# Seven block products: low parts of w_out2 on GpSimd, one weight difference kept in its block's place

## The chip, the cores and the metric

The kernel runs on one core of a Trainium2 chip. The metric is device time in microseconds (us), from the first to the last instruction plus what lies around the program. The engines are named as the profile names them: PE (TensorE matmuls), PEld (its weight loads), DVE (VectorE), ACT (ScalarE), POOL (GpSimd) and SP (the queue that issues DMAs).

## The reference

Three stages in a row: attention with a mask of hash buckets, a bilinear block, and a gated block. The change lies in the third.

```python
# attention: 2 batches x 8 heads, 768 positions, head size 64 -> x of 1536 x 512
h = (x @ w1) * (x @ w2) @ w3;  x = h @ w_out                 # d_ff 1024
gate = 1 / (1 + exp(-(x @ w_gate)));  val = x @ w_val        # d_ff 1536
return (gate * val) @ w_out2                                 # 1536 x 512
```

The inputs are drawn as double precision and are brought to 32 bits on the chip.

## The kernel before

**Precision.** A matrix operand is split into a high part (a rounded copy made by ACT) and a low part (the operand minus the high part, one subtraction of two SBUF operands). A product of two operands is three matmuls: high by high, high by low, low by high. `three` (L705) issues them, `split_w` (L699) and `low` (L778) make the two parts.

**The gated block** is computed for three sweeps of 512 tokens, each over twelve tiles of 128 hidden units. The first sweep multiplies plainly. The last two go through `sevens`, which takes two tiles at a time (a *pair*; six pairs a sweep, twelve in all) and makes each 2 by 2 block product of weights and tokens with seven block products in place of eight, for `w_gate` (k = 0) and `w_val` (k = 1). It needs sums and differences of weight blocks. With B11 and B21 the two blocks of a pair's even tile, and B12 and B22 those of its odd tile:

- `t1` makes B12 - B11 on DVE, into a scratch tile `r1`;
- `t24` makes B22 - (B12 - B11), and B21 minus that, in a scratch tile (`r24`, shown as `xlf`), and splits the two (`wh`, `wl`);
- `t3` makes B22 - B12 (also shown as `xlf`) and splits it and B22 (`da`, `dr`);
- `t1low` splits `r1`, both k in one step of 128x512 (`st`);
- `own` splits the even tile itself (`wah`, `wal`, `wbh`, `wbl`).

The low parts of all of these are made on POOL, the differences themselves on DVE. The seven products of a pair go to halves of the PSUM tiles `pa` and `pb`, and DVE adds each to sums in SBUF (`add`, L882; tiles `a` and `xhf`), which frees the bank for a later product. A gated tile is finished by L945 or L965 (value times gate), a high part on ACT (`gh`) and a low part on DVE (`gl`, L922).

**The second matmul** (`second`, tiles `m`) multiplies a gated tile by its 128 rows of w_out2, four token blocks of three matmuls each. These steps are spread between the seven products. The w_out2 rows are split just before: the high part `wth` on ACT, the low part `wtl` on DVE (L699, since `split_w` is called with `eng=dve`), two buffers.

**Order.** The weights lie in SBUF from the first sweep on (tiles `xall`, `w1r`, `w2r` and `wc`, each in reused space), and nothing is loaded any more in the last two sweeps. Within each engine the instructions stand in a fixed order, which a scheduler lays out from the written order, priorities and its own estimate of times; an instruction whose operands are late holds up what stands behind it on its engine. The work for pair p + 1 is written between the products of pair p.

Of the kernel before, what the change touches and what calls it, by code (L numbers as in the profile page):

```python
# [10 lines left out]
F32 = mybir.dt.float32  # L11
# [218 lines left out]
def lsh_attention_moe_moe2_kernel(  # L230
# [22 lines left out]
    P = 128  # L253
# [8 lines left out]
    CH = 512  # L262
# [8 lines left out]
    dve = nc.vector  # L271
    pool = nc.gpsimd
# [3 lines left out]
    def act_copy(dst, src):  # L276
        act.activation(out=dst, in_=src, func=AF.Copy)  # L277

    def f(ap):
        return ap.bitcast(F32)  # L280
# [409 lines left out]
    def split_w(pl, nm, src, bufs=2, eng=pool):  # L690
        hi = pl.tile([P, DM], F32R, tag=nm + "h", name=nm + "h", bufs=bufs)
        lo = pl.tile([P, DM], F32R, tag=nm + "l", name=nm + "l", bufs=bufs)
        shp = src.shape
        h3, l3 = hi, lo
        if len(shp) == 3:
            h3 = hi.rearrange("p (k f) -> p k f", k=shp[1])
            l3 = lo.rearrange("p (k f) -> p k f", k=shp[1])
        act_copy(h3, src)
        eng.tensor_tensor(out=l3, in0=src, in1=f(h3), op=ALU.subtract)  # L699
        return hi, lo  # L700
# [11 lines left out]
    def ftile(fi):  # L712

        ck, o = divmod(fi, KC)
        g = xall[:, o, ck * CH:(ck + 1) * CH].rearrange("p (k f) -> p k f", k=KC)
        if fi < NF1:
            return g, late["w1"][fi], late["w2"][fi].rearrange("p k f -> p (k f)")
        return g, wc[:, fi - NF1].rearrange("p (k f) -> p k f", k=KC), wc[:, fi - NF1 + KC]

    def moe(psM):  # L720


        tiles = [(1, s, fi) for s in range(1, NSW) for fi in range(NF1)] + [(2, s, fi) for s in range(NSW) for fi in range(NF2)]
        mp, mw = late["mp"], late["mw"]
# [51 lines left out]
        def low(eng, hi, lo, src):  # L776
            act_copy(hi, src)
            eng.tensor_tensor(out=lo, in0=src, in1=f(hi), op=ALU.subtract)  # L778
# [22 lines left out]
        def sevens():  # L801
# [3 lines left out]
            NS = NF2 // 2  # L805
            pairs = [(s, NF1 * (NSW - 1) + s * NF2 + 2 * i) for s in range(1, NSW) for i in range(NS)]
# [4 lines left out]
            h1 = [sts[3][:, i * DM:(i + 1) * DM] for i in range(2)]  # L811
# [5 lines left out]
            h24 = [[mw.tile([P, DM], F32R, tag=t, name=t, bufs=3) for t in ("wh", "wl")] for _ in range(3)]  # L817
            hb3 = [[pl.tile([P, DM], F32R, tag=t, name=t, bufs=b) for t in ("da", "dr")] for pl, b in ((mp, 2), (mp, 2), (dec, 1))]
            W = [{}, {}]
            r1, r24 = (mp.tile([P, CH], F32, tag="o", name="tmp", bufs=2) for _ in range(2))  # L820
            r24 = [r24, None]

            def raw(p, k):
                fi = tiles[pairs[p][1]][2]
                return [fl(t) for t in (ftile(fi)[k][:, 0:2], ftile(fi + 1)[k][:, 0:2], ftile(fi)[k][:, 2:4], ftile(fi + 1)[k][:, 2:4])]

            def sub(o, a, b):
                dve.tensor_tensor(out=o, in0=a, in1=b, op=ALU.subtract)  # L828

            def t1(p):  # L830

                if p < len(pairs):
                    for k in range(2):
                        b11, b12, _, _ = raw(p, k)
                        sub(r1[:, k * 2 * P:(k + 1) * 2 * P], b12, b11)

            def t24(p, k):

                if p < len(pairs):
                    _, _, b21, b22 = raw(p, k)  # L840
                    h, l = h24[(2 * p + k) % 3]
                    r = r24[k]
                    sub(r[:, :2 * P], b22, r1[:, k * 2 * P:(k + 1) * 2 * P])
                    sub(r[:, 2 * P:], b21, r[:, :2 * P])
                    low(pool, h, l, r)
                    W[p % 2][k, 6], W[p % 2][k, 4] = [[half(t, i) for t in (h, l)] for i in range(2)]

            def t3(p, k):

                if p < len(pairs):  # L850
                    _, b12, _, b22 = raw(p, k)
                    h, l = hb3[(2 * p + k) % 3]
                    r = r3[:, k * 2 * P:(k + 1) * 2 * P]
                    sub(r, b22, b12)
                    low(pool, h[:, :2 * P], l[:, :2 * P], r)
                    low(pool, h[:, 2 * P:], l[:, 2 * P:], b22)
                    W[p % 2][k, 7], W[p % 2][k, 3] = [[half(t, i) for t in (h, l)] for i in range(2)]

            def t1low(p):
                if p < len(pairs):  # L860
                    low(pool, *h1, r1)
                    for k in range(2):
                        W[p % 2][k, 5] = [half(t, k) for t in h1]

            def own(p, k):
# [6 lines left out]
            def product(p, k, i):  # L872

                q = (7 * p + place[i]) % 4
                r = banks[k][q % 2][:, q // 2 * 2 * P:(q // 2 + 1) * 2 * P]
                w, x = W[p % 2][k, i], X[i]
                for kk in range(2):
                    three(r, [t[:, kk] for t in w], [t[:, kk] for t in x], kk == 0, kk == 1)
                return r
# [9 lines left out]
            xf = [mw.tile([P, KC, CH], F32, tag=t, name=t + "f") for t in ("xh", "xl")]  # L889
# [4 lines left out]
            t24(0, 1)  # L894
            t3(0, 1)
            t1low(0)
            r1, r24[0] = xf[0][:, 2], xf[1][:, 0]
            yield
            banks = [[psM.tile([P, 512], F32, tag=t, name=t) for t in ("pa", "pb")] for _ in range(2)]
            todo = [(pairs[0][1] - 1, c) for c in range(4)]  # L900
# [1 line left out]
            for p, (s, n) in enumerate(pairs):  # L902
                if p == NS:
                    X = {**nextX, **S}
                elif p == NS - 2:
                    nextX, nextS = blocks(2, [xf[0][:, 3], xf[1][:, 3]] + [mp.tile([P, CH], F32, tag="o", name="tmp", bufs=2) for _ in range(2)])

                def renew(i):
                    if p == NS - 1:
                        low(dve, *S[i], nextS[i])  # L910
                A = [mp.tile([P, CH], F32, tag="a", name="a", bufs=2) for _ in range(2)]
                C = [A, vs]

                def sec():
                    if todo:
                        second(*todo.pop(0))

                def gate(i):
                    gh = mw.tile([P, CH], F32R, tag="gh0", name="gh", bufs=2)
                    gl = mw.tile([P, CH], F32R, tag="gl0", name="gl", bufs=2)  # L920
                    act_copy(gh, vs[i])
                    dve.tensor_tensor(out=gl, in0=vs[i], in1=f(gh), op=ALU.subtract)  # L922
                    gs[n + i] = gh, gl

                for k in range(2):
                    act_copy(C[k][0][:, hi2], product(p, k, 1))
                for k in range(2):
                    add(C[k][1][:, lo2], product(p, k, 6), C[k][0][:, hi2])
                renew(6)
                sec()  # L930
                if p:
                    wts[n - 1] = split_w(mp, "wt", ftile(tiles[n - 1][2])[2], eng=dve)
                for k in range(2):
                    add(C[k][0][:, lo2], product(p, k, 2), C[k][0][:, hi2])
                sec()
                for k in range(2):
                    add(C[k][1][:, hi2], product(p, k, 7), C[k][1][:, lo2])
                renew(7)
                own(p + 1, 0)
                sec()  # L940
                for k in range(2):
                    add(C[k][0][:, hi2], product(p, k, 4), C[k][1][:, hi2])
                    if k == 0:
                        act.activation(out=A[0], in_=A[0], func=AF.Sigmoid)
                dve.tensor_tensor(out=vs[0], in0=vs[0], in1=A[0], op=ALU.mult)  # L945
                gate(0)
                own(p + 1, 1)
                t1(p + 1)
                t24(p + 1, 0)
                sec()  # L950
                wts[n] = split_w(mp, "wt", ftile(tiles[n][2])[2], eng=dve)
                sec()
                for k in range(2):
                    r = product(p, k, 5)
                    add(C[k][1][:, hi2], r, C[k][1][:, hi2])
                    add(C[k][1][:, lo2], r, C[k][1][:, lo2])
                renew(5)
                t3(p + 1, 0)
                sec()
                t24(p + 1, 1)  # L960
                for k in range(2):
                    add(C[k][1][:, lo2], product(p, k, 3), C[k][1][:, lo2])
                    if k == 0:
                        act.activation(out=A[1], in_=A[1], func=AF.Sigmoid)
                dve.tensor_tensor(out=vs[1], in0=vs[1], in1=A[1], op=ALU.mult)  # L965
                gate(1)
                sec()
                t3(p + 1, 1)
                t1low(p + 1)
                sec()  # L970
                todo = [(n + i, c) for i in range(2) for c in range(4)]
            n = pairs[-1][1] + 1
# [5 lines left out]
        gs, wts = {}, {}  # L978
# [40 lines left out]
    o = D // 2  # L1019
# [120 lines left out]
```

## Time and profile before

| what | value |
|---|---|
| median of three runs | 833.38 us (832.77 to 836.6) |
| the profiled execution | 834.98 us, span 833.2 us |
| granted PE clock over the span | 0.995 |
| PE busy | 795.7 us (96%) |
| DVE busy | 669.3 us (80%) |
| ACT busy | 546.3 us (66%) |
| POOL busy | 414.7 us (50%) |

Busy times are unions of an engine's instructions. A group of equal instructions has its number, its mean duration and the idle time of the engine just ahead of it with what ended that idle time. The first sweep of the gated block ends and `sevens` begins its preparations at about 602 us; the products of its first pair start at 621 us, and the last matmul ends at 829.3 us.

### The profile page before, as it was taken

The page shows a single profiled execution, that of the slowest core. Times are in us where ns is not written, and L with a number is a line of the kernel's source. Part 1 is how long each engine was busy: PE and PEld are TensorE (multiplying, and loading weights), DVE is VectorE, ACT ScalarE, POOL GpSimd, SP SyncE. Part 2 cuts the span into 40 slices and gives each one's busy share as a digit, 9 for nine tenths or more (in the row PEclk, how much of TensorE's full clock was granted, in tenths as well). Part 3 has the DMA queues.
Part 4 walks back from the last instruction along what each step waited for, and adds up shares of the span by engine and source line. Part 5 has one row for each costly group of instructions (what it writes and reads, how often), then busy time and mean ns, then how long its engine had stood idle before and what let it go on. Part 6 is the DMA issues. An engine that isn't in the chain of part 4 may idle for free.

```text
span 833.2 us, 13347 instructions
## 1 busy us (share of the span) xinstructions
PE 795.7 (96%) x4576; PEld 684.3 (82%) x4576; DVE 669.3 (80%) x1217; ACT 546.3 (66%) x1085; POOL 414.7 (50%) x420
## 2 busy tenths in 40 slices
PE   6898999999999999999999999999998999899998
PEld 5677888888788888888888888888877889798996
DVE  6869989888799989977376545686799988988874
ACT  6888878777787888876455645656545455555542
POOL 3466443232565464438344434446557566656640
PEclk9999999999999999999999999999999999999999
DMA  6866645344455545130022213334101000010001
GB/s 230 209 193 174 184 121 157 88 121 121 116 140 148 137 124 147 61 111 1 1 77 76 77 52 125 103 113 141 50 1 52 1 1 1 1 52 1 1 1 52
DMA packets 45956, 74.19 MB, mean 89 GB/s; under 512 B 6336, under 2 KB 32960, under 8 KB 45888
## 3 DMA queue, kind: packets, MB, share of 16 engines
q1 hardware_dynamic: 45888, 73.34, 30.3%
q8 instruction: 36, 0.59, 0.3%
q14 instruction: 32, 0.26, 0.1%
HBM read 52.43 MB, written 3.19 MB: 67 GB/s over the span
## 4 chain that ended last, share of the span: by engine, by line
PE 60%; DVE 22%; ACT 6%; issue 6%; DMA 3%; POOL 2%; SPq 0%; ACTq 0%; DVEq 0%; POOLq 0%
PE m L705 11%; PE pa L705 10%; PE pb L705 10%; PE av L541 7%; PE tp L523 4%; PE wacc L600 4%; PE p L705 4%; DVE s L479 3%; PE s L469 3%; PE s L472 2%; PE y L705 2%; DVE pt L528 2%; DVE da L338 2%; DVE xlf L828 2%; PE gps L402 2%
## 5 line engine op out<-in xcount | busy, mean ns | idle before, releaser
L523 PE MATMUL tp<-idf,e 128*128 128x128 f32 x576 | 102.9, 276 | 5.3 <-DVE pt L528 4.9
L336 POOL TENSOR_SCALAR da<-da 128x512 f32<-128x512 f32 x76 | 52.5, 693 | 111.5 <-ACT da L334 110.3
L490 ACT ACTIVATE e<-s,sm 128x768 f32<-128x768 f32 x96 | 95.7, 999 | 15.9 <-DVE sm L480 15.4
L526 ACT ACTIVATE pt<-tp 128x384 fp32r<-128x384 f32 (+1 forms) x192 | 89.9, 493 | 20.7 <-PE tp L523 18.3
L479 DVE TENSOR_REDUCE s<-s 128x1 f32<-128x768 f32 x96 | 91.2, 955 | 11.9 <-PE s L472 10.7
L528 DVE TENSOR_TENSOR pt<-tp,pt 128x384 fp32r<-128x384 f32 x168 | 87.9, 548 | 4.1 <-ACT pt L526 2.9
L523 PEld LDWEIGHTS tp<-idf,e 128*128 128x128 f32 x576 | 71.4, 141 | 19.3 <-DVE pt L528 6.3
L541 PE MATMUL av<-pt,spv 128*128 128x256 f32 (+1 forms) x576 | 85.2, 297 | 1.7 <-DVE pt L528 1.5
L334 ACT ACTIVATE da<-st 128x512 f32<-128x512 f32 x76 | 51.1, 672 | 52.7 <-DVE w1r L343 20.2
L541 PEld LDWEIGHTS av<-pt,spv 128*128 128x128 f32 (+1 forms) x576 | 72.7, 182 | 11.0 <-DVE pt L528 2.4
L469 PE MATMUL s<-bk,bq 128*128 128x384 f32 x192 | 62.8, 389 | 6.4 <-ACT e L490 6.1
L600 PE MATMUL wacc<-wo,t 128*128 128x512 f32 x192 | 64.1, 415 | 1.7 <-DVE pt L528 1.6
L338 DVE SCALAR_TENSOR_TENSOR da<-st,da 128x512 uint32<-128x512 uint32 x76 | 59.6, 785 | 1.2
L705 PE MATMUL m<-wth,gh 128*128 128x512 f32 x144 | 57.4, 399 | 3.0 <-ACT gh L277 2.9
L705 PE MATMUL m<-wtl,gh 128*128 128x512 f32 x144 | 57.1, 396 | 0.0
L472 PE MATMUL s<-ak,aq 128*128 128x384 f32 x192 | 56.5, 360 | 0.0
L705 PE MATMUL pa<-x,wah 128*128 128x512 f32 (+1 forms) x176 | 48.9, 361 | 3.1 <-DVE a L882 3.1
L335 ACT ACTIVATE dr<-st 128x512 int32<-128x512 uint32 x76 | 50.7, 668 | 0.0
L705 PE MATMUL pb<-x,wbh 128*128 128x512 f32 (+1 forms) x176 | 48.5, 360 | 0.0
L778 POOL TENSOR_TENSOR wl<-xlf,wh 128x512 fp32r<-128x512 f32 x23 | 33.4, 1455 | 30.2 <-ACT wh L277 30.2
L705 PE MATMUL m<-wth,gl 128*128 128x512 f32 x144 | 48.5, 394 | 0.0
L745 DVE TENSOR_TENSOR pb<-pb,a 128x512 f32<-128x512 f32 x28 | 19.5, 695 | 35.5 <-PE pb L705 28.2
(245 smaller groups left out, 2352.6 us busy)
## 6 DMA issues: line engine op xcount, KB each, us to landing
st<-in_moe_w_dram SPq DMA_DIRECT2D x32, 512.0 KB, 4.0
st<-in_moe_w_out_dram SPq DMA_DIRECT2D x20, 512.0 KB, 4.1
st<-in_moe_w_gate_dram SPq DMA_DIRECT2D x12, 512.0 KB, 3.5
st<-in_moe_w_val_dram SPq DMA_DIRECT2D x12, 512.0 KB, 3.6
rawq<-in_q_dram SPq DMA_DIRECT2D x16, 192.0 KB, 3.7
rawk<-in_k_dram SPq DMA_DIRECT2D x16, 192.0 KB, 3.4
rr<-row SPq DMA_DIRECT2D x16, 192.0 KB, 3.4
out_dram<-o SPq DMA_DIRECT2D x12, 256.0 KB, 2.1
```

What stands on the lines that cost most here:

```text
L336: pool.tensor_scalar(out=f(a), in0=f(a), scalar1=F64_HI, scalar2=F64_LO, op0=ALU.min, op1=ALU.max)
L338: dve.scalar_tensor_tensor(out=a, in0=hw, scalar=0xC0000000, in1=a, op0=ALU.bitwise_and, op1=ALU.bitwise_or)
L469: pe.matmul(s[:, half, :HS], lhsT=m["bq"][:, qs], rhs=m["bk"][:, ks], start=True, stop=False)
L472: pe.matmul(s[:, half, :HS], lhsT=m["aq"][:, qs], rhs=m["ak"][:, ks], start=False, stop=True)
L479: dve.tensor_reduce(out=one[:, 1:2], in_=s[:, :, :HS], op=ALU.max, axis=AX.XY, negate=True)
L490: act.activation(out=e.rearrange("p (a c) -> p a c", a=2), in_=s[:, :, :HS], func=AF.Exp, bias=sm[:, 1:2], scale=sm[:, 0:1], accum_out=su_ ...
L523: pe.transpose(ps[:, j * P:(j + 1) * P], e[:, c * P:(c + 1) * P], idf)
L526: act.activation(out=dh, in_=src, func=AF.Copy)
L528: dve.tensor_tensor(out=d, in0=src, in1=f(dh), op=ALU.subtract)
L541: pe.matmul(acc[:w.shape[1], :2 * P].rearrange("p (a t) -> p a t", a=2), lhsT=w, rhs=r[:, :, c], start=(c == 0 and i == 0), stop=(c == NT ...
L600: pe.matmul(acc, lhsT=t3[x][:, j], rhs=wo[y][:, j], start=(j == 0 and n == 0), stop=(j == NF1 - 1 and n == 2))
L705: mm = pe.matmul(ps, lhsT=lhs[x], rhs=rhs[y], start=start and n == 0, stop=stop and n == 2)
```

## The change

Two edits in `sevens`.

First, 23 calls of `split_w` for w_out2 rows lose `eng=dve`, so that their low parts `wtl` are made on POOL (the default). The first sweep's calls and the call for the very last tile keep DVE.

Second, `t1` writes B12 - B11 over B12 itself. Since the first of the two sweeps in `sevens` leaves it there, `t1` runs for that sweep's six pairs only. `r1` is gone; `t24` reads the block in its place; `t3` takes B22 - B12 as (B22 - (B12 - B11)) - B11, from the half that `t24` has just made; and `t1low` splits each k by itself, two steps of 128x256 in place of one of 128x512.

```diff
             def t1(p):
-                if p < len(pairs):
+                if p < NS:
                     for k in range(2):
                         b11, b12, _, _ = raw(p, k)
-                        sub(r1[:, k * 2 * P:(k + 1) * 2 * P], b12, b11)
+                        sub(b12, b12, b11)
...
-                    _, _, b21, b22 = raw(p, k)
+                    _, b12, b21, b22 = raw(p, k)
-                    sub(r[:, :2 * P], b22, r1[:, k * 2 * P:(k + 1) * 2 * P])
+                    sub(r[:, :2 * P], b22, b12)
...
-                    sub(r, b22, b12)
+                    sub(r, r24[k][:, :2 * P], b11)
...
             def t1low(p):
-                    low(pool, *h1, r1)
                     for k in range(2):
+                        h, l = (t[:, k * 2 * P:(k + 1) * 2 * P] for t in h1)
+                        low(pool, h, l, raw(p, k)[1])
...
                 if p:
-                    wts[n - 1] = split_w(mp, "wt", ftile(tiles[n - 1][2])[2], eng=dve)
+                    wts[n - 1] = split_w(mp, "wt", ftile(tiles[n - 1][2])[2])
...
-                wts[n] = split_w(mp, "wt", ftile(tiles[n][2])[2], eng=dve)
+                wts[n] = split_w(mp, "wt", ftile(tiles[n][2])[2])
```

The scheduler lays the instructions out anew. On DVE, where the first sweep of `sevens` passes into the second, there stood before:

```order
L882 TENSOR_TENSOR a<-pb,a 128x256
L778 TENSOR_TENSOR st_6938<-xhf,st_6938 128x512
L828 TENSOR_TENSOR xlf<-w1r_2782 128x256
L882 TENSOR_TENSOR xhf<-pb,xhf 128x256
L699 TENSOR_TENSOR wtl<-wc,wth 128x512
L828 TENSOR_TENSOR xlf<-xall 128x256
L882 TENSOR_TENSOR a<-pa,a 128x256
L945 TENSOR_TENSOR xhf<-xhf,a 128x512
L882 TENSOR_TENSOR a<-pa,a 128x256
```

and in the changed kernel, at the same place (its `sub` is L827):

```order
L882 TENSOR_TENSOR a<-pb,a 128x256
L778 TENSOR_TENSOR st_6938<-xhf,st_6938 128x512
L882 TENSOR_TENSOR xhf<-pb,xhf 128x256
L945 TENSOR_TENSOR xhf<-xhf,a 128x512
L827 TENSOR_TENSOR xlf<-w1r_2782 128x256
L882 TENSOR_TENSOR a<-pa,a 128x256 x2
L882 TENSOR_TENSOR xhf<-pa,xhf 128x256 x2
```

The `wtl` and one difference have left the place ahead of the two reads of `pa`, and L945 stands earlier.

In the first pair, DVE had these rows between a multiplication by the gate (L745, the last plain tile) and the first addition of a product (L882) before:

```order
L828 TENSOR_TENSOR xhf<-xall 128x256
L828 TENSOR_TENSOR xhf<-w1r_2782,w1r_2781 128x256
L787 TENSOR_TENSOR xhf<-x_0_2_5062,x_1_2_5063 128x512
L828 TENSOR_TENSOR xlf<-w1r_2779,xlf 128x256
L828 TENSOR_TENSOR xlf<-xall 128x256
L828 TENSOR_TENSOR xlf<-xall,xhf 128x256
L748 TENSOR_TENSOR gl<-pb,gh 128x512
L699 TENSOR_TENSOR wtl<-w2r_2787,wth 128x512
L787 TENSOR_TENSOR xlf<-xlf,xhf 128x512
L828 TENSOR_TENSOR xlf<-w1r_2782 128x256
L828 TENSOR_TENSOR xlf<-xall,xlf 128x256
L882 TENSOR_TENSOR a<-pb,a 128x256
```

and in the changed kernel:

```order
L787 TENSOR_TENSOR xhf<-x_0_2_5062,x_1_2_5063 128x512
L827 TENSOR_TENSOR xlf<-w1r_2779,xlf 128x256
L827 TENSOR_TENSOR xlf<-xlf,w1r_2779 128x256
L827 TENSOR_TENSOR xlf<-xall,xlf 128x256
L827 TENSOR_TENSOR xlf<-xlf,xall 128x256
L787 TENSOR_TENSOR xlf<-xlf,xhf 128x512
L748 TENSOR_TENSOR gl<-pb,gh 128x512
L882 TENSOR_TENSOR a<-pb,a 128x256
```

Eleven rows ahead of L882 have become seven: the next pair's `t1` (two rows `xhf`), the `wtl` and the next pair's first differences no longer stand there. (L787 makes token sums, `xlf` and `xhf` being scratch for them too.)

On POOL, the steps for one pair of the second sweep stood so before (`st` is `t1low`, `wl` is `t24`, `dr` is `t3`):

```order
L778 TENSOR_TENSOR wl<-xlf,wh 128x512
L699 TENSOR_TENSOR wal<-xall,wah 128x512
L699 TENSOR_TENSOR wbl<-w1r_2781,wbh 128x512
L778 TENSOR_TENSOR dr<-xlf,da 128x256 x2
L778 TENSOR_TENSOR wl<-xlf,wh 128x512
L778 TENSOR_TENSOR st_6939<-xhf,st_6939 128x512
L778 TENSOR_TENSOR dr<-w1r_2780,da 128x256
L778 TENSOR_TENSOR dr<-xall,da 128x256
```

and in the changed kernel, for the same pair:

```order
L699 TENSOR_TENSOR wtl<-wc,wth 128x512
L699 TENSOR_TENSOR wal<-xall,wah 128x512
L699 TENSOR_TENSOR wbl<-w1r_2781,wbh 128x512
L778 TENSOR_TENSOR dr<-xlf,da 128x256 x2
L778 TENSOR_TENSOR wl<-xlf,wh 128x512
L699 TENSOR_TENSOR wtl<-wc,wth 128x512
L778 TENSOR_TENSOR wl<-xlf,wh 128x512
L778 TENSOR_TENSOR st_6939<-xall,st_6939 128x256
L778 TENSOR_TENSOR st_6939<-w1r_2780,st_6939 128x256
L778 TENSOR_TENSOR dr<-w1r_2780,da 128x256
L778 TENSOR_TENSOR dr<-xall,da 128x256
```

The first `wl` has moved behind the two `dr<-xlf`, and a `wtl` stands in its old place and another between the two `wl`.

## Rows read from the trace of the kernel before

**Rows 1.** Page, part 1: busy time, share of the span and instructions of each engine

```profile
PE 795.7 (96%) x4576; PEld 684.3 (82%) x4576; DVE 669.3 (80%) x1217; ACT 546.3 (66%) x1085; POOL 414.7 (50%) x420
```

**Rows 2.** Windows (us): each engine's busy time (instructions), granted PE clock, DMA share, GB/s

```profile
520.00:606.00 86.00, 86.00 (x381) 71.25 (x380) 63.02 (x97) 52.07 (x94) 43.13 (x41) 1.00 0.32 101
606.00:634.00 28.00, 24.52 (x128) 20.50 (x126) 27.30 (x38) 15.25 (x32) 17.68 (x14) 1.00 0.00 1
634.00:660.00 26.00, 23.62 (x156) 20.72 (x156) 25.49 (x49) 14.65 (x30) 17.12 (x15) 1.00 0.11 41
660.00:720.00 60.00, 59.27 (x401) 54.56 (x402) 53.99 (x106) 32.83 (x67) 39.77 (x34) 1.00 0.00 1
720.00:730.00 10.00, 7.46 (x43) 6.59 (x42) 10.00 (x20) 4.02 (x9) 5.07 (x5) 0.83 0.00 0
730.00:800.00 70.00, 68.28 (x467) 63.03 (x466) 59.20 (x118) 38.63 (x76) 43.19 (x37) 1.00 0.05 16
```

**Rows 3.** Waits of PE from 590 us on: us in total, times, longest; longest of five

```profile
PE pa L705 <- DVE a L882: 3.9, 3, 2.5
```

**Rows 4.** Timeline of PE: start, us, instruction, count, [idle before <- what ended it]

```profile
625.00 0.50 PE L705 MATMUL m<-wth,gh 128*128 128x512 f32 x1 [1.62 <-ACT gh L277]
...
631.78 0.50 PE L705 MATMUL pb<-st,da 128*128 128x256 f32 x2 [1.60 <-DVE a L882]
...
725.06 0.51 PE L705 MATMUL pa<-x,wah 128*128 128x256 f32 x2 [2.54 <-DVE a L882]
...
727.03 0.63 PE L705 MATMUL m<-wtl,gh 128*128 128x512 f32 x1
...
734.01 0.40 PE L705 MATMUL m<-wtl,gh 128*128 128x512 f32 x1
```

**Rows 5.** Timeline of DVE in the first pair, and at the change of sweeps

```profile
627.11 1.39 DVE L699 TENSOR_TENSOR wtl<-w2r,wth 128x512 fp32r<-128x512 f32 x1
...
629.57 1.49 DVE L828 TENSOR_TENSOR xlf<-w1r 128x256 f32<-128x256 f32 x1
...
631.32 0.41 DVE L882 TENSOR_TENSOR a<-pb,a 128x256 f32<-128x256 f32 x1
...
719.46 0.96 DVE L828 TENSOR_TENSOR xlf<-w1r 128x256 f32<-128x256 f32 x1
720.34 0.41 DVE L882 TENSOR_TENSOR xhf<-pb,xhf 128x256 f32<-128x256 f32 x1
720.68 1.45 DVE L699 TENSOR_TENSOR wtl<-wc,wth 128x512 fp32r<-128x512 f32 x1
722.05 1.49 DVE L828 TENSOR_TENSOR xlf<-xall 128x256 f32<-128x256 f32 x1
723.47 0.41 DVE L882 TENSOR_TENSOR a<-pa,a 128x256 f32<-128x256 f32 x1
...
724.60 0.41 DVE L882 TENSOR_TENSOR a<-pa,a 128x256 f32<-128x256 f32 x1
```

**Rows 6.** Timelines of DVE and POOL from 707 to 710 us

```profile
707.38 1.65 DVE L699 TENSOR_TENSOR wtl<-wc,wth 128x512 fp32r<-128x512 f32 x1
...
707.19 1.29 POOL L778 TENSOR_TENSOR st<-xhf,st 128x512 fp32r<-128x512 f32 x1 [2.69 <-ACT st L277]
708.45 1.18 POOL L778 TENSOR_TENSOR dr<-wc,da 128x256 fp32r<-128x256 f32 x1
709.59 0.74 POOL L778 TENSOR_TENSOR dr<-xall,da 128x256 fp32r<-128x256 f32 x1
```

**Rows 7.** Groups by line and shape, 606 to 834 us: busy us, mean ns | idle before

```profile
L778 POOL TENSOR_TENSOR wl<-xlf,wh 128x512 fp32r<-128x512 f32 x23 | 33.4, 1455 | 30.2 <-ACT wh L277 30.2
L778 POOL TENSOR_TENSOR dr<-xlf,da 128x256 fp32r<-128x256 f32 x24 | 21.4, 900 | 7.3 <-ACT da L277 6.1 <-PE pa L705 1.1
L699 DVE TENSOR_TENSOR wtl<-w2r,wth 128x512 fp32r<-128x512 f32 x16 | 16.2, 1014 | 1.9 <-ACT wth L277 1.9
L828 DVE TENSOR_TENSOR xhf<-xall 128x256 f32<-128x256 f32 x11 | 8.3, 752 | 0.0
```

More of the change, by code (lines that the diff above doesn't have):

```diff
@@ L819, in sevens @@
             W = [{}, {}]
-            r1, r24 = (mp.tile([P, CH], F32, tag="o", name="tmp", bufs=2) for _ in range(2))
-            r24 = [r24, None]
+            r24 = [mp.tile([P, CH], F32, tag="o", name="tmp", bufs=2), None]
             def raw(p, k):
@@ L850, in t3 @@
                 if p < len(pairs):
-                    _, b12, _, b22 = raw(p, k)
+                    b11, _, _, b22 = raw(p, k)
                     h, l = hb3[(2 * p + k) % 3]
                     r = r3[:, k * 2 * P:(k + 1) * 2 * P]
-                    sub(r, b22, b12)
+                    sub(r, r24[k][:, :2 * P], b11)
                     low(pool, h[:, :2 * P], l[:, :2 * P], r)
@@ L896, in sevens @@
             t1low(0)
-            r1, r24[0] = xf[0][:, 2], xf[1][:, 0]
+            r24[0] = xf[1][:, 0]
             yield
```

## Prediction

> **What bounds the kernel now.** I read the page's busy shares first: PE is busy 96% of the span [rows 1], so only the places where it is not busy can give anything back. The windows say where these are [rows 2]. From 520 to 606 us PE is busy all of the time; from 606 on, in the stretch that the change touches, it idles 28.00 - 24.52 = 3.48 us, then 2.38, 0.73, 2.54 and 1.72 us, together 10.85 us up to 800 us. The same rows show the reason: DVE is busy 27.30 of 28 us, 25.49 of 26 and 10.00 of 10 just where PE idles most, while POOL is busy 17.68, 17.12 and 5.07 us there. The list of waits agrees: the dearest wait of PE is for DVE to add a product and so to free its bank [rows 3]. The timeline shows the three big gaps [rows 4]: 1.62 us at 625 us (for a high part on ACT, itself behind DVE), 1.60 us at 631.78 us and 2.54 us at 725.06 us, the last where the first sweep of seven products passes into the second. After that one the granted clock in the 10 us window is 0.83 [rows 2], which means that PE ran 0.17 x 10 / 0.5 = 3.4 us at the lower of its two levels (1.2 GHz) after it had idled; a 512-column matmul there takes 0.63 us and later 0.40 us [rows 4]. That costs another 1.7 us. So at most 10.85 + 1.7 = 12.6 us can come back up to 800 us, and DVE's queue decides.
>
> **What the change takes from DVE.** 23 subtractions of 128x512 leave it, at a mean of 1.01 us [rows 7]: 23.3 us. The differences `t1` of the second sweep vanish, and those of the first move ahead, into the plain sweep. In the stretch from 606 us on there are 22 of them; eleven took 0.752 us in the mean [rows 7], and the other eleven cost at least what a 128x256 operation of DVE takes unhindered, 0.41 us [rows 5]: 8.3 + 4.5 = 12.8 us. Of DVE's 148.7 busy us from 634 to 800 us (90% of 166) some 30 go, and it comes down to about 70%.
>
> The twelve differences that move ahead cost 12 x 0.41 = 4.9 us, or 18 us if each took the 1.49 us of the slowest one shown [rows 5]. They fall where DVE is busy 63.02 of 86 us and PE never waits [rows 2]. I take nothing for them; 18 us is still inside the 23 us that DVE has free there, and its cover would be gone only if one stood right ahead of an operation for which PE waits, 1.5 us at the worst.
>
> **What it puts on POOL.** 23 subtractions at 1.29 us unhindered [rows 6] to 1.455 us in the mean [rows 7]: 30 to 33 us. `t1low` in two halves costs 2 x 0.90 - 1.455 = 0.35 us more, twelve times: 4 us. POOL is busy 105.2 of 166 us between 634 and 800 us (63%) and gets about 31 more there: 82%. It has the room: 30 us of its idle time is spent ahead of `wl` waiting for ACT [rows 7], which is where the new order puts a `wtl`. A result can also come late without harm: the low part that DVE made at 720.68 us is first read by PE at 734.01 us [rows 4, 5], so a queue of several microseconds on POOL is covered. What stands behind a late `wtl` in POOL's queue are the `dr` of the next pair, and behind these the differences on DVE that overwrite their scratch, and then the additions that free PE's banks. ACT makes one copy more a pair (two halves for one); it is busy 38.63 of 70 us [rows 2], which covers it.
>
> **The places.** In the first pair, a `wtl` of 1.39 us and a difference of 1.49 us stood ahead of the addition at 631.32 us for which PE waited 1.60 us [rows 4, 5]. In the new order neither is ahead of it: 2.88 us are gone, and the wait with them. I count 1.6 us.
> At the change of sweeps, a `wtl` of 1.45 us and a difference of 1.49 us stood ahead of the two additions from `pa` [rows 5]; both are now behind. Start to start they held DVE from 720.68 to 723.47 us, 2.79 us, and PE's gap was 2.54 us. I count 2.54 us, and 1.7 us for the clock: the two gaps of 1.6 us in the first pair left it at 1.00 [rows 2], so that what is left of this one should not lower it. Together 4.2 us.
> The 1.62 us at 625 us stay, since the same four operations stand ahead of it on DVE in both orders.
> The rest up to 800 us, 10.85 - 1.62 - 1.60 - 2.54 = 5.1 us in many small gaps, are waits of the same kind, with DVE 20 points less busy. I count half, 2.5 us; the bounds are 0 and 5.1.
>
> **What stands against it.** First, a subtraction of DVE with two SBUF operands and one of POOL do not run side by side here: the `wtl` that DVE began at 707.38 us took 1.65 us and ended at 709.03, 0.55 us after POOL's step that had begun at 707.19; the next step of POOL then took 1.18 us where the one behind it took 0.74 [rows 6]. Each moved subtraction therefore holds up the other engine for 1.29 us in place of some 0.55 us. The Trainium skill (SBUF — State Buffer, Who interferes with whom) states it as an exclusive lock: a VectorE instruction with two SBUF inputs and a GpSimd instruction that reads SBUF exclude each other for the whole of the one that began first. The trace agrees with it [rows 6], and by it this change lengthens the sum of holds.
> DVE keeps ten such subtractions a pair of fourteen, so the fewer of them meet a POOL that is busy more often: 10 x 0.82 against 14 x 0.63, 8.2 against 8.8 meetings. I take it as even within a pair, and charge 2 us for new waits behind POOL (between 0 and the rival below). Second, in the last pair the one `wtl` that stays on DVE now stands ahead of the last gated tile: 0.6 us.
>
> **The sum.** 1.6 + 4.2 + 2.5 - 2.0 - 0.6 = 5.7 us. The profiled execution took 834.98 us (its span 833.2 and 1.8 around it), so 829.3 us for such a one. The median of the runs is 833.38 us, 1.6 us below it; the forecast for a median is **827.7 us**.
>
> **The rivals.**
> *Slower: the shared access to SBUF sets the pace.* Per pair, in the steady part, DVE held it for six operations of 128x512 at 0.55 us and eight of 128x256 at half that, 5.5 us, and POOL for five at 1.29 and four at 0.74, 9.4 us: 14.9 us. POOL does nine steps a pair, 91 from 634 to 800 us [rows 2], so that 10.1 pairs lie there: 16.4 us each, of which PE's gaps (7.4 us) and the clock (1.7 us) make 0.9; PE alone needs 15.5 us. With the change DVE holds the access 4 x 0.55 + 6 x 0.28 = 3.9 us and POOL 6 x 1.29 + 6 x 0.74 = 12.2 us: 16.1 us. From the point where this sum passes PE's 15.5 us, PE waits for it. Packed end to end it would still end 0.3 us below the 16.4 of now; if the holds kept today's ratio to the pair (16.4 over 14.9), a pair would take 17.7 us. The middle is 17.0, 0.6 us more than now: 11 pairs that prepare a next one, 7 us, 833.4 + 7 = 840 us. For it: the sum passes the bound by 4%. Against it: operations overlap a little at their ends (DVE's next starts 0.07 us before its last is over [rows 5]), and PE ran 59.27 of 60 us with the sum at 14.9.
> *No change: the waits move to POOL.* The gap at the change of sweeps closes, and as much comes up elsewhere, because the `dr` and `wl` of a pair come later behind the `wtl`. 834.98 - 1.6 - 4.2 + 4 = 833 us. For it: POOL at 82%, in a fixed order. Against it: the room ahead of `wl`.
> *More: all the waits on DVE go,* the one at 625 us too, and POOL costs nothing: 833.4 - 12.6 = 821 us.
> *The change does not do what it says* in one way: a block overwritten early would have to wait for its last readers in the plain sweep, and hold DVE's queue there. PE has no gap there that would show such a wait to be near [rows 2], and the price would be at most 1.5 us; it has no case of its own.
>
> **How the numbers follow.** Forecast 0.55 (its own range 823 to 831), no change 0.25, slower 0.12, more 0.08. A measurement of this kernel can tell about 0.5% from no change, 4.2 us, so "faster" ends at 829.2 us. Of the forecast's share some 0.46 lies below that and 0.09 above; with the case of more this gives 0.54 faster; 0.34 the same (0.25 and 0.09); 0.12 slower. The range for 8 in 10 leaves out most of the slower case and the far end of the case of more: 821 to 836 us.
>
> **What would show each step.** No gap of PE over 1 us between 650 and 800 us, and a clock of 1.00 through the change of sweeps, show the two places right. DVE near 70% and POOL near 82% busy from 634 to 800 us show the counts right. If PE's waits name POOL, or DVE's waits for `dr` grow from few to many microseconds, the second rival holds; if DVE's remaining subtractions take over 1 us in the mean while POOL's grow beyond 1.5 us, the first does. The prediction is wrong if PE's idle time from 634 to 800 us does not shrink although DVE's does.

## The result: slower by 1%

The changed kernel took 842.88 us (median; 842.37 to 843.63) beside 834.96 us for the kernel before on the same chip: a ratio of 1.0106, with a 95% interval of 1.0085 to 1.0128. I had forecast 827.7 us with a range of 821 to 836. The profiled execution took 843.06 us with a span of 841.2, which is 8.0 us more than before.

The windows of the changed kernel, with the columns of [rows 2] and at the same places:

```profile
520.00:606.00 86.00, 86.00 (x381) 71.21 (x380) 67.40 (x107) 53.58 (x97) 46.61 (x43) 1.00 0.33 104
606.00:634.00 28.00, 24.65 (x126) 20.36 (x124) 26.35 (x36) 14.90 (x31) 20.02 (x15) 1.00 0.04 16
634.00:660.00 26.00, 18.61 (x113) 16.33 (x114) 24.01 (x39) 10.95 (x23) 17.00 (x15) 0.93 0.07 25
660.00:720.00 60.00, 56.38 (x382) 51.22 (x380) 46.58 (x84) 31.39 (x65) 47.53 (x44) 1.00 0.00 1
720.00:730.00 10.00, 9.66 (x69) 9.11 (x70) 7.53 (x17) 6.90 (x14) 6.52 (x7) 1.00 0.01 2
730.00:800.00 70.00, 67.45 (x459) 61.42 (x458) 57.98 (x102) 38.69 (x83) 56.85 (x51) 1.00 0.05 16
```

PE idles 3.35 + 7.39 + 3.62 + 0.34 + 2.55 = 17.25 us from 606 to 800 us, where it idled 10.85 us before [rows 2]: 6.4 us of the 8.0. (Some 0.9 us lie in the attention, and 0.5 us at the end.) DVE has 50 instructions fewer from 634 to 800 us (240 for 290), but its busy time fell only from 148.7 to 136.1 us: those that stayed take longer.

The waits of PE from 600 us on (us in total, times, longest), with [rows 3] for their like before. The three longest are shown. The engine waited for is DVE, above all with the additions that free banks (L882), and not POOL:

```profile
PE pb L705 <- DVE xhf L882: 4.9, 5, 2.0
PE pb L705 <- DVE a L882: 4.4, 1, 4.4
PE m L705 <- DVE gl L922: 2.8, 3, 1.2
```

The largest gap, 4.37 us, shows why. First PE, then DVE, then POOL in the timeline of the changed kernel:

```profile
654.80 0.74 PE L705 MATMUL pb<-x,wh 128*128 128x256 f32 x2 [4.37 <-DVE a L882]
...
648.60 1.45 DVE L827 TENSOR_TENSOR xlf<-w1r,xlf 128x256 f32<-128x256 f32 x1
649.97 1.49 DVE L827 TENSOR_TENSOR xlf<-xlf,w1r 128x256 f32<-128x256 f32 x1
651.39 1.75 DVE L787 TENSOR_TENSOR tmp<-xlf,tmp 128x512 f32<-128x512 f32 x1
...
654.33 0.41 DVE L882 TENSOR_TENSOR a<-pb,a 128x256 f32<-128x256 f32 x1
...
648.48 1.29 POOL L699 TENSOR_TENSOR wal<-xall,wah 128x512 fp32r<-128x512 f32 x1 [1.62 <-ACT wah L277]
649.72 1.47 POOL L699 TENSOR_TENSOR wtl<-w2r,wth 128x512 fp32r<-128x512 f32 x1
651.15 1.44 POOL L699 TENSOR_TENSOR wbl<-w1r,wbh 128x512 fp32r<-128x512 f32 x1
```

Three DVE operations that take 0.41, 0.41 and 0.68 us when POOL is idle took 1.45, 1.49 and 1.75: each began while a POOL step was under way and ended 0.28, 0.27 and 0.55 us behind that step's end, and the next two POOL steps took 1.47 and 1.44 us in place of 1.29. The addition at 654.33 us stands behind all three. Three such operations that stand there undisturbed take 1.27 us from the first's start to the next row's (653.06 to 654.33 us in the same trace); these took 4.46 us (648.60 to 653.06). So some 3.2 us of the gap come from the meeting, an estimate, and the rest from the length of the queue. The granted clock fell after this gap (0.93 from 634 to 660 us), where before it had fallen after the 2.54 us gap [rows 2, 4].

In this gap, then, the price is paid where differences (L827) and block sums (L787) stand on DVE ahead of additions and meet POOL. Open was which half of the change does it, and through what.

### The profile page after: what moved, and what is told of

The parts are those of the page before. It is cut to its first block, busy times and chain, and to the rows that moved or that the text cites. A ratio compares the mean times of both kernels' runs of the same rounds, so it can differ in the third digit from the quotient of the medians.

```text
span 841.2 us, 13399 instructions
## 1 busy us (share of the span) xinstructions
PE 795.9 (95%) x4576; PEld 683.4 (81%) x4576; DVE 660.4 (79%) x1182; ACT 546.7 (65%) x1097; POOL 449.9 (53%) x455
## 4 chain that ended last, share of the span: by engine, by line
PE 73%; DVE 17%; ACT 3%; issue 3%; POOL 2%; DMA 1%; SPq 0%; ACTq 0%; DVEq 0%; POOLq 0%
PE pb L705 14%; PE m L705 14%; PE pa L705 13%; PE av L541 7%; PE tp L523 5%; PE wacc L600 4%; DVE xlf L827 4%; PE p L705 4%; PE s L469 3%; PE s L472 3%; DVE s L479 3%; PE y L705 2%; PE gps L402 2%; DVE pt L528 2%; DVE da L338 1%
## 5 line engine op out<-in xcount | busy, mean ns | idle before, releaser
L705 PE MATMUL m<-wth,gl 128*128 128x512 f32 x144 | 51.4, 397 | 2.9 <-DVE gl L922 2.8
L745 DVE TENSOR_TENSOR pb<-pb,a 128x512 f32<-128x512 f32 x28 | 19.5, 695 | 38.7 <-PE pb L705 35.2
L469 PEld LDWEIGHTS s<-bk,bq 128*128 128x128 f32 x192 | 33.9, 193 | 17.1 <-ACT e L490 13.3
```

Source lines behind the costliest of these rows:

```text
L469: pe.matmul(s[:, half, :HS], lhsT=m["bq"][:, qs], rhs=m["bk"][:, ks], start=True, stop=False)
L705: mm = pe.matmul(ps, lhsT=lhs[x], rhs=rhs[y], start=start and n == 0, stop=stop and n == 2)
```

## The experiments

**Each half alone.** The first kernel is the kernel before with the 23 low parts on POOL; the second the changed kernel with them back on DVE.

```diff
-wts[n] = split_w(mp, "wt", ftile(tiles[n][2])[2], eng=dve)     # and wts[n - 1]: low parts on POOL alone
+wts[n] = split_w(mp, "wt", ftile(tiles[n][2])[2])
```

> The kernel before, with the 23 low parts of w_out2 moved to POOL and nothing else (the differences t1 stay as they were, in r1, for all twelve pairs). Theory 1 (the shared access to SBUF: POOL holds it for 1.29 us for each moved subtraction where DVE held it for about 0.55, and DVE's differences and block sums stand still for it, with the additions that free PE's banks behind them): this half alone carries the loss, 841 to 850 us, with DVE's subtractions of 128x512 near 1.5 us or more where POOL works back to back. Theory 2 (the loss comes from the in-place differences, which read what other steps just wrote and have a longer chain for t3): this half alone is a gain or nothing, 829 to 835 us.

Measured: 838.12 us, 1.0042 of before [1.0028, 1.0056]. A loss, but between the two expectations, and under half of the whole. DVE's differences lengthen here too, from 0.61 us in the mean to 0.69 between 634 and 800 us (54.8 us for 80, from the groups by shape); the ten `xlf<-xall` took 1.31 us, where nine had taken 0.80.

> The changed kernel with the 23 low parts of w_out2 made on DVE again: B12 - B11 in its block's place, and nothing else of the change. Theory 1 (shared access to SBUF): DVE loses twelve differences net of the stretch of the seven products and POOL only gets t1low in two halves, 4 us in all beside other work, so 829 to 834 us, no slower than the kernel before. Theory 2 (the in-place differences cost): 840 us or more, with PE waiting for additions that stand behind the new t3.

Measured: 844.94 us, 1.0121 [1.0094, 1.0149]. The prediction counts on a gain from this half. The half that only takes work away from DVE is the dearer one, and as slow as both together (the two intervals overlap). PE's waits of this kernel (same columns as above):

```profile
PE pa L705 <- DVE a L882: 4.6, 4, 2.0
PE pa L705 <- DVE xhf L882: 4.1, 7, 2.2
PE pb L705 <- DVE xhf L882: 2.1, 3, 1.1
```

The sum of holds doesn't explain it, since this kernel has less of them: from 620 to 800 us, the time in which POOL or an operation of DVE with two SBUF operands was under way (the union of their recorded spans in the trace) is 154.8 us, against 165.8 before and 165.5 in the changed kernel.

**No low parts at all.** The changed kernel and the kernel before, each without the 23 subtractions (`eng=None`: the high part stands in for the low).

> The changed kernel without the 23 subtractions for w_out2's low parts on any engine: the high part is multiplied in place of the low part, so that part of the computation is changed; the matmuls are as many as before. It shows what these subtractions cost on POOL beside nothing at all. Theory 1 (shared access to SBUF): all of the loss goes and more, 824 to 830 us, and the 4.4 us gap of PE at 655 us shrinks to below 1 us. Theory 3 (the loss comes from where the scheduler now puts the block sums and differences on DVE, ahead of the additions that free PE's banks, not from POOL's holds): that order stays much the same, so it stays at 838 us or above.

> The kernel before without the 23 subtractions for w_out2's low parts (the high part is multiplied in place of the low part, so that part of the computation is changed): the price of these subtractions on DVE. The changed kernel without them took 834.3 us. Theory 4 (the in-place half costs 8 to 10 us whatever becomes of the low parts): 824 to 828 us. If it takes 832 us or more, the low parts on DVE cost nothing and the in-place half costs only with them.

Measured: 834.32 us, 0.9995 [0.9985, 1.0004], and 827.42 us, 0.9915 [0.990, 0.993]. The first lies between the two expectations. The second agrees with theory 4 as its expectation states it: the in-place half costs 6.9 us without any low parts, beside 10.2 us with them on DVE and some 4.8 us with them on POOL. The 23 subtractions cost 7 us on DVE in the kernel before.

**Block sums later.** The changed kernel; the sums of the last sweep (L787; there are eight of them, not seven as the expectation has it) wait for the fourth pair's last addition.

```diff
-nextX, nextS = blocks(2, [...
+with tc.issue_after(late['added']): nextX, nextS = blocks(2, [...
```

> The changed kernel, with one edit of order: the seven block sums of the last sweep (L787, 128x512 each, which the scheduler puts among the first two pairs of the seven products, from 623 to 656 us) may not start on DVE before the last addition of the fourth pair. Theory 3 (what stands on DVE ahead of the additions in the first two pairs makes the loss): PE's gaps from 625 to 657 us, 10.5 us in all, and the lower clock behind them (1.7 us) mostly go: 831 to 835 us. Theory 1 (shared access to SBUF, the sum of holds of DVE and POOL in every pair): the gaps only move to where the sums now lie, 840 us or more.

Measured: 843.58 us, 1.0110 [1.0087, 1.0132]. PE idled 1.1 us in place of 7.4 from 634 to 660 us, and 7.1 in place of 3.6 from 660 to 720: the gaps moved with the sums. Theory 3, that the crowd in the first pairs alone makes the loss, falls.

**The wait that went with r1.** In the kernel before, `t1` of the next pair writes r1, which POOL's step `st` of this pair reads. So `t1`, and `t24` behind it, cannot come ahead of `st`. DVE and POOL in the kernel before:

```profile
745.76 1.07 DVE L965 TENSOR_TENSOR xhf<-xhf,a 128x512 f32<-128x512 f32 x1 [0.25 <-ACT a L964]
746.75 0.96 DVE L828 TENSOR_TENSOR xhf<-xall 128x256 f32<-128x256 f32 x1
747.63 0.41 DVE L828 TENSOR_TENSOR xhf<-w1r,w1r 128x256 f32<-128x256 f32 x1
747.97 0.41 DVE L828 TENSOR_TENSOR xlf<-xall,xhf 128x256 f32<-128x256 f32 x1
...
744.98 1.30 POOL L778 TENSOR_TENSOR st<-xhf,st 128x512 fp32r<-128x512 f32 x1
746.23 1.20 POOL L778 TENSOR_TENSOR dr<-xall,da 128x256 fp32r<-128x256 f32 x1
750.73 1.35 POOL L778 TENSOR_TENSOR wl<-xlf,wh 128x512 fp32r<-128x512 f32 x1 [3.30 <-ACT wh L277]
```

Behind `st` and `dr` POOL has nothing to do for 3.30 us, since it waits for ACT's copies of these very differences: five of the six (two of `t1`, four of `t24`) ran unhindered at 0.41 us there. In the in-place kernel no such wait holds `t24` back. DVE, POOL and PE of the in-place kernel (`xlf<-xall,xlf` is of `t24`, `xlf<-xlf,xall` of `t3`, which reads what `t24` has made):

```profile
661.25 0.64 DVE L827 TENSOR_TENSOR xlf<-xall,xlf 128x256 f32<-128x256 f32 x1
661.81 0.96 DVE L827 TENSOR_TENSOR xlf<-xlf,xall 128x256 f32<-128x256 f32 x1
662.70 1.21 DVE L945 TENSOR_TENSOR xhf<-xhf,a 128x512 f32<-128x512 f32 x1
663.82 0.74 DVE L882 TENSOR_TENSOR xhf<-pa,xhf 128x256 f32<-128x256 f32 x2
...
660.88 0.74 POOL L778 TENSOR_TENSOR dr<-w1r,da 128x256 fp32r<-128x256 f32 x1
661.57 0.93 POOL L778 TENSOR_TENSOR st<-w1r,st 128x256 fp32r<-128x256 f32 x1
662.45 0.90 POOL L778 TENSOR_TENSOR dr<-xall,da 128x256 fp32r<-128x256 f32 x1
...
664.62 0.50 PE L705 MATMUL pa<-x,wbh 128*128 128x256 f32 x2 [2.21 <-DVE xhf L882]
```

They now stand among POOL's short steps, and the additions at 663.82 us behind them: PE waited 2.21 us for these. The test is to put `t24` back behind L965 by order alone, in both kernels:

```diff
+x = dve.tensor_tensor(out=vs[1], in0=vs[1], in1=A[1], op=ALU.mult).ins          # L965
+for y in late["t24"]: tc.add_manual_dep(y, x.name, ...NoSync...)     # t24 of pair p + 1, on DVE
```

> The changed kernel with one edit of order: the four differences of t24 for the next pair may not start on DVE before L965 of the pair ahead. In the kernel before, t1 had to wait for POOL's step st on r1, and with it t24, so that these differences ran in one block behind L965 while POOL waited for ACT, 0.41 us each (746.75 to 750.32 us there). Without r1 they stand among POOL's five short steps and the additions. Theory 4 (the lost wait on r1 is what costs: differences now meet POOL and hold up the additions behind them): most of the 8 us go, 834 to 838 us, with the low parts of w_out2 on POOL still costing a few us. Theory 1 (sum of holds): no change, 841 to 845 us.

> The same edit of order on the kernel with the in-place difference alone (low parts of w_out2 on DVE). That kernel took 844.9 us with less work on DVE than before. Theory 4 (place of the differences): 829 to 836 us, 8 us or more below the same kernel without the edit. Theory 5 (the in-place form costs by itself: the longer chain of t3, t1low in two halves): it stays at 840 us or above.

Measured: 834.76 us, 1.0008 [0.9998, 1.0018], for the whole change; 827.91 us, 0.9919 [0.9903, 0.9935], for the in-place half. The order of four differences a pair is worth 8 and 17 us (the two of `t3` go behind L965 with them, since they read what `t24` has made). Three groups of differences on DVE from 634 to 800 us (busy, mean ns), of the in-place kernel and then of the same with the order:

```profile
L827 DVE TENSOR_TENSOR xlf<-xlf,xall 128x256 f32<-128x256 f32 x10 | 7.9, 793 | 0.0
L827 DVE TENSOR_TENSOR xlf<-xall,xlf 128x256 f32<-128x256 f32 x10 | 7.5, 751 | 0.0
L827 DVE TENSOR_TENSOR xlf<-w1r 128x256 f32<-128x256 f32 x6 | 5.5, 916 | 0.5 <-POOL wl L778 0.4
```

```profile
L827 DVE TENSOR_TENSOR xlf<-xlf,xall 128x256 f32<-128x256 f32 x10 | 5.2, 521 | 0.0
L827 DVE TENSOR_TENSOR xlf<-xall,xlf 128x256 f32<-128x256 f32 x10 | 4.1, 412 | 0.0
L827 DVE TENSOR_TENSOR xlf<-w1r 128x256 f32<-128x256 f32 x7 | 2.9, 412 | 0.0
```

Two more kernels put the wait to the test in the kernel before: r1 in two places in turn (so that the wait goes), and `t1` held behind L965 (so that it is stricter).

```diff
-sub(r1[:, k * 2 * P:(k + 1) * 2 * P], b12, b11)
+sub(r1[p > NS and p % 2][:, k * 2 * P:(k + 1) * 2 * P], b12, b11)       # r1 = [xf[0][:, 2], xf[0][:, 3]]
```

> The kernel before, with one edit: in the second sweep of the seven products r1 has two places in turn (the other is a scratch that is free there), so that t1 and t24 need no longer wait for POOL's step on r1. Nothing is computed otherwise, and there is more room. Theory 4 (that wait kept the differences out of POOL's way): the differences move up among POOL's steps and the additions, PE's gaps from 730 to 800 us (1.7 us before) grow by 2 to 4 us: 836 to 839 us. Theory 5: no change, 833 to 835.5 us.

> The kernel before, with t1 (and so t24 behind it) of the next pair not before L965 of the pair ahead: the same edit of order as for the in-place kernel, which then took 827.9 us. In the kernel before, the wait on r1 already puts most of these differences there. If the gain of that kernel comes from the in-place form (fewer differences): 833 to 836 us here, little changed. If it comes from the order alone: 826 to 830 us here too.

Measured: 837.62 us, 1.0027 [1.0012, 1.0043], and 838.51 us, 1.0052 [1.0034, 1.0070]. More room made the kernel before slower, by as much as expected, but not where it was expected. At the change of sweeps two rows of `t1` moved up from 726.53 to 721.43 us, and PE's gap there grew from 2.54 us [rows 4] to 3.74:

```profile
721.43 1.18 DVE L828 TENSOR_TENSOR xhf<-xall 128x256 f32<-128x256 f32 x1
722.54 0.41 DVE L828 TENSOR_TENSOR xhf<-w1r,w1r 128x256 f32<-128x256 f32 x1
722.87 1.76 DVE L699 TENSOR_TENSOR wtl<-wc,wth 128x512 fp32r<-128x512 f32 x1
724.55 0.94 DVE L828 TENSOR_TENSOR xlf<-xall 128x256 f32<-128x256 f32 x1
725.42 0.41 DVE L882 TENSOR_TENSOR a<-pa,a 128x256 f32<-128x256 f32 x1
...
727.01 0.50 PE L705 MATMUL pa<-x,wah 128*128 128x256 f32 x2 [3.74 <-DVE a L882]
```

In the pairs behind this place the differences moved up as well (the next two times that `t1` runs it starts at 728.81 and 749.32 us, where it was 746.75 and 762.40), but PE idled only 2.25 us from 730 to 800 us, for 1.72 before and 4.01 in the in-place kernel. So the lost wait, taken away in the second sweep alone, is shown to let the differences move up and to cost 3 us; that it makes the whole 10 us of the in-place half is not shown.

The other kernel, with `t1` held behind L965, missed its range (833 to 836) on the high side. With `t1` in the chain, six differences and then ACT's copy and POOL's `wl` have to fit between L965 and the next pair's products, and PE waited for POOL (2.1 us in all) and for `gh` (5.7 us). So the order alone is no gain; it is one for the in-place form. That this is because its chain is two differences shorter is argued, not shown.

**Why the meeting is dear: reads of SBUF.** The changed kernel with `t24` behind L965, and in it POOL's 23 subtractions made memsets of the same tile, so that these low parts are zero:

```diff
-eng.tensor_tensor(out=l3, in0=src, in1=f(h3), op=ALU.subtract)
+[pool.memset(f(l3), 0.0) for _ in range(3)] if nm == "wt" and eng is pool else eng.tensor_tensor(...)
```

> The changed kernel with t24 behind L965 (834.8 us), and on POOL three memsets of the low part's tile in place of each of the 23 subtractions (the low part is left at zero, so that part of the computation is changed): POOL has as much to do or more, in its queue at the same places, but these instructions read nothing from SBUF, and they don't wait for ACT's high part. DVE's order is the same but for a few rows. If it is the shared access to SBUF that makes the low parts on POOL dear: 822 to 829 us, with DVE's subtractions shorter. If it is POOL's queue, with wl and dr late behind the low parts: 833 us or more.

Measured: 827.05 us, 0.9905 [0.9886, 0.9923], in place of 834.76. DVE's rows are the same in both kernels here; with the subtraction (DVE, then POOL), and then with the memsets:

```profile
625.53 1.51 DVE L827 TENSOR_TENSOR xlf<-xlf,w1r 128x256 f32<-128x256 f32 x1
626.96 1.75 DVE L787 TENSOR_TENSOR xlf<-xlf,xhf 128x512 f32<-128x512 f32 x1
...
625.37 1.38 POOL L699 TENSOR_TENSOR wtl<-w2r,wth 128x512 fp32r<-128x512 f32 x1
```

```profile
625.27 0.41 DVE L827 TENSOR_TENSOR xlf<-xlf,w1r 128x256 f32<-128x256 f32 x1
625.61 0.68 DVE L787 TENSOR_TENSOR xlf<-xlf,xhf 128x512 f32<-128x512 f32 x1
...
625.02 1.11 POOL L699 MEMSET wtl<- 128x512 f32 x2
```

Beside a POOL step that reads SBUF the difference takes 1.51 us, beside one that only writes 0.41. That is what the Trainium skill (SBUF — State Buffer, Who interferes with whom) states: a VectorE instruction with two SBUF inputs contends with a GpSimd instruction that reads SBUF and not with one that only writes it. The memsets also spare POOL the wait for ACT's high part, so not all of the 7.7 us need be the access; the two operations above are. To see whether the mere place ahead of the additions costs anything, the in-place kernel (844.94 us) had all of POOL's subtractions in the stretch replaced in the same way, by three memsets for 128x512 and two for 128x256:

> The in-place difference alone, without any edit of order (844.9 us): all of POOL's subtractions in the stretch of the seven products are memsets of the same tiles, three for 128x512 and two for 128x256 (their low parts are left at zero, so that part of the computation is changed). POOL has about as much to do, but reads nothing from SBUF. The differences stand ahead of the additions as before. If what they cost there is the wait for POOL's hold: 822 to 830 us, each difference at its 0.41 us. If their place ahead of the additions costs by itself: 838 us or more.

Measured: 821.57 us, 0.9851 [0.9838, 0.9865]. The groups of DVE's differences from 634 to 800 us, and PE's window there:

```profile
L827 DVE TENSOR_TENSOR xlf<-xlf,xall 128x256 f32<-128x256 f32 x9 | 3.8, 423 | 0.0
L827 DVE TENSOR_TENSOR xlf<-xall,xlf 128x256 f32<-128x256 f32 x9 | 3.8, 422 | 0.0
...
660.00:720.00 60.00, 59.98 (x412) 55.55 (x412) 43.39 (x103) 35.95 (x73) 35.06 (x91) 1.00 0.00 1
```

Nothing was reordered by hand (the scheduler put some differences even further ahead), and the loss is gone. The memsets also spare POOL its waits for ACT, and POOL is busy 90.5 us from 634 to 800 us in place of 103.7. But in the in-place kernel DVE waited only 0.4 us there for a result of POOL, and no wait of PE names POOL. What is left is that DVE's operations are short again: the place costs little by itself, and nearly all by the access that the engines share.

**Does POOL's longer hold cost in every pair?** With `t24` in its place, the low parts on POOL still cost 834.76 - 827.91 = 6.9 us, most of it ahead of 660 us: by the windows from 606 to 660 us PE idled 4.1 us more than with the low parts on DVE, and the clock of 0.87 in place of 0.93 from 634 to 660 us is another 0.06 x 26 = 1.6 us, while from 660 to 720 us PE was busy 59.74 of 60 us. So the block sums were moved again, first together behind the fourth pair, then two a pair behind `t24` of the first four pairs:

> The in-place difference alone with t24 behind L965 (827.9 us), and the block sums of the last sweep not before the last addition of the fourth pair. In that kernel 4.4 us of PE's 6.2 us of gaps lie at 623 to 648 us, where these sums (L787) stand on DVE among the first pair's additions and ahead of L965 and the differences behind it, and the granted clock falls there (0.93 from 634 to 660 us). If it is the crowding of the first pairs, and the later pairs have room: 822 to 826 us. If the sums cost as much wherever they lie (as they did in the changed kernel without the order of t24): 827 to 830 us.

> The changed kernel (low parts of w_out2 on POOL and in-place difference) with both edits of order: t24 behind L965, block sums later. With t24 behind L965 alone it took 834.8 us, PE idled 0.3 us in all from 660 to 720 us although POOL and DVE's subtractions together filled all of that time, and all of its loss against the kernel with the low parts on DVE lay in the first pairs. Theory A (the low parts on POOL cost only where DVE is crowded as well): 822 to 829 us, as with the low parts on DVE. Theory 1 (the sum of holds, now with the sums on top in later pairs that are already full): 832 us or more, with PE's gaps where the sums now lie.

> The in-place difference alone (low parts of w_out2 on DVE), t24 behind L965, and the eight block sums of the last sweep spread: two a pair behind the differences of t24, in the first four pairs. Held together to the fifth pair, they made 4.2 us of gaps there and 0.94 of the clock over 60 us; among the first pair they made as much. If it is crowding at one place: PE's gaps from 622 to 730 us fall from 6 us to 2 us and the clock stays at 1.00: 821 to 825 us. If eight sums cost the same wherever they are (each holds up an addition): 827 to 829 us.

> The whole change (low parts of w_out2 on POOL and the in-place difference) with both edits of order, the sums two a pair. Crowding: 821 to 826 us, within 2 us of the same kernel with the low parts on DVE, since POOL's longer holds show only where DVE is crowded. Sum of holds: POOL's longer holds cost in every pair, 4 us or more above the same kernel with the low parts on DVE.

Measured: sums together 828.59 us, 0.9925 [0.9909, 0.9941], with the low parts on DVE, and 830.10 us, 0.9941 [0.9921, 0.9960], on POOL; spread 823.93 us, 0.9884 [0.9866, 0.9903], and 825.29 us, 0.9896 [0.9881, 0.9910]. Moving the heap alone gained nothing with the low parts on DVE (827.91 us without it) and 4.7 us with them on POOL (834.76 without it); spreading the sums gained another 4.7 and 4.8 us. The windows of the last kernel, the whole change with both edits of order:

```profile
634.00:660.00 26.00, 26.00 (x172) 23.78 (x171) 21.79 (x43) 14.80 (x32) 20.86 (x19) 1.00 0.00 1
660.00:720.00 60.00, 57.35 (x392) 52.56 (x391) 48.64 (x94) 31.58 (x67) 52.65 (x45) 1.00 0.00 1
730.00:800.00 70.00, 69.74 (x483) 65.14 (x484) 49.88 (x111) 36.98 (x79) 54.71 (x51) 1.00 0.02 6
```

POOL is busier from 634 to 800 us than in the changed kernel (136.3 us for 127.9), and PE is busy 162.8 of the 166 us. The two intervals overlap: with the sums spread, it no longer shows on which engine the low parts are made. All medians together (us; the kernel before had 834.0 to 835.0 beside each; the in-place kernel with all of POOL's subtractions as memsets, 821.57, stands outside):

| | low parts on DVE | on POOL | left out, or memsets |
|---|---|---|---|
| r1, as before | 834 to 835 | 838.12 | 827.42 |
| in place | 844.94 | 842.88 (the change) | 834.32 |
| in place, t24 behind L965 | 827.91 | 834.76 | 827.05 |
| the same, sums in one heap later | 828.59 | 830.10 | |
| the same, sums spread | **823.93** | 825.29 | |

## Why the prediction was wrong, step by step

**What bounds the kernel** was right: DVE's queue ahead of the additions decides, and PE's waits name it first in the changed kernel and in each half alone (not with `t1` held behind L965, where `gh` of ACT comes first).

**What the change takes from DVE** is the step that failed. I counted `t1` as 12.8 us of busy time and nothing else. It also carried a wait, on r1 until POOL had read it, and behind that wait `t24` stood out of POOL's way. The change took away both; the in-place half alone then cost 10 us in place of gaining. That the place of `t24` costs this is shown, since the order alone gives back 17 us there and 8 us in the whole change. That the wait is what had kept the place is shown in part: two places for r1 cost the kernel before 3 us. DVE's fall to 70% did not come either: 82%, since its differences grew from 0.61 us in the mean (48.0 us for 79 from 634 to 800 us, summed from the groups by shape) to 0.88 (53.4 us for 61), where 0.41 is what they take unhindered.

**What stands against it**: "even within a pair" was the same error in another place. I let ten operations meet POOL in proportion to its busy share, 8.2 meetings against 8.8, as if their places were random. They are not: before, the differences fell into POOL's idle time (3.30 us in the pair shown), and after, into its steps. The same error holds for the 23 low parts: moved alone they cost 3.4 us in place of a gain. The row on the shared access [rows 6] was read rightly. The 2.0 us charged for it were too little, and they are not waits behind POOL's results as I put it, but waits of DVE for access.

**The places.** The wait of 1.60 us in the first pair went as forecast, but gaps of 1.17, 1.52, 2.02 and 4.37 us from 630 to 655 us took its place. At the change of sweeps the gap shrank to 1.26 us (I had 0) and the clock stayed at 1.00 there, as forecast; the fall of the clock only moved, behind the 4.37 us gap. The 1.62 us at 625 us stayed (1.42). Of the 2.5 us from the small gaps nothing came.

**What came as forecast.** The twelve differences that moved ahead of 606 us cost nothing (PE 86.00 of 86 us there, DVE 67.40), the tail cost 0.46 us (0.6), and POOL's 77% from 634 to 800 us was near the 82%. I had written that no gap over 1 us from 650 to 800 us would show the places right; there are five. The last sign that I had named for a wrong prediction came true too: PE's idle time from 634 to 800 us did not shrink, it grew from 7.4 to 13.9 us.

**The rivals.** "Slower: the shared access sets the pace" had the right side and nearly the time (840 us; the middle of its two values is 16.9 us a pair and not 17.0, so 839), but not the mechanism; that it came so near is luck. It made the sum of holds per pair the bound. The in-place half alone, with the least of such time of the three kernels compared above, is as slow as the whole change, and the last kernel runs at 825 us although such operations are under way for 175 of the 180 us from 620 to 800 us. Which operation meets which, and what stands behind it, decides.

## What to carry to other kernels

A buffer's reuse can also be an order: before a scratch tile is removed, look at what its wait kept apart, and put the order back by hand if it did something. Where two engines exclude each other on SBUF, don't count holds; look in the trace for the other engine's idle stretch and put the operations there, above all those ahead of what frees PSUM banks. A list of optional work (here eight block sums) is spread over the pairs, not left where the scheduler first finds room.

## What was not expected of the hardware

Beside POOL steps back to back, DVE's subtractions and POOL's steps took turns one for one, and an operation of 0.41 us took 1.45 us and one of 0.68 us 1.75 (648 to 653 us in the changed kernel): the wait is inside the recorded duration, so that DVE looks busy, and the idle time ahead of its rows shows nothing. And it is POOL's reading that excludes: two memsets of POOL, 1.11 us, held up neither of the two DVE operations beside them (625.02 to 626.29 us in the kernel with memsets).
